# Scatters that no longer wait for each other, and one gather put behind a branch, in the last pairs of a routed expert kernel

## The chip, the cores and the metric

The kernel runs on one core of a Trainium2 chip. The metric is device time in microseconds; the time before is the median of 6 runs. One more execution was profiled, and every reading of the profile below is from that one. TensorE is called PE, VectorE DVE, ScalarE ACT, GpSimd POOL and SyncE SP. "PEld" is PE's loading of weights, and a "q" behind an engine's name (POOLq) means its instruction queue: branches, waits on semaphores, issues of DMAs.

## The reference

The inputs are `x` (8 batches, 8 heads, 512 tokens, 64 wide), a `state` of 32 rows per head, and the weights of 8 experts. First comes a small attention in both directions, which gives 544 rows of 512 per batch:

```python
xread = softmax(x @ state.T * scale) @ state
sread = softmax(state @ x.T * scale) @ x
x = concat([xread, sread])          # (8, 544, 512) after the heads are joined
```

Then every row passes through one of the experts:

```python
logits = x @ w_gate                                  # (8, 544, 8)
local_gate = sigmoid(x @ w_local)
for s in range(S):
    fresh_e = argmax(logits[b, s])
    e = fresh_e if s == 0 or local_gate[b, s] < 0.5 else prev_e
    prev_e = e
    p = softmax(logits[b, s])
    h = max(x[b, s] @ w1[e], 0)                      # 512 -> 1024
    out[b, s] = p[e] * (h @ w2[e])                   # 1024 -> 512
```

There are 4352 rows in all. The change touches only the second part, where rows are gathered by expert, multiplied with that expert's two matrices, and scattered back to their places in `out`.

## The kernel before

The first part of the kernel (the first 130 us or so) computes the attention and the routing: it writes the rows to a DRAM tensor `rows` and works out, on the chip, which row goes to which slot. Slots are dealt to experts in *pairs* of two blocks of 128 rows. How many pairs there are depends on the data; a number between `NPMIN` = 10 and `NP` = 23 is read into a register, `pairs`. Rows that don't fill a pair are handled by small tiles of 32 rows, one beside each of the first nine pairs.

The pairs 0 to 8 are written out as straight code (the loop that calls `pair(u, True, ...)`). From pair 9 on the function `last` takes over: it calls `pair(u, ..., late=False)`, and the next pair stands inside `tc.If(pairs > u + 1)`, so that it runs only if it exists. These are the conditional pairs of this text. With the inputs at hand the 32 scatters of the profile show 16 pairs, so pairs 9 to 15 run in this form; pair 15 is the last, and behind it each engine takes its branch to the end of the kernel.

A pair does two products by a scheme with seven instead of eight block products (a Strassen scheme). The function `seven` writes their order out by hand: products 1, 5, 6, 2, 3, 7, 4 in the second half of a conditional pair (`apart=True`). The first half (`strassen`) makes the hidden layer from the transposed rows `x_t` and the weights `a`; the second half (`second_half`) makes the output from the hidden layer and the weights `c`. PE runs the block products; ACT and DVE copy the results out of PSUM, scale them by the row's probability, and add them up into two output tiles: `ys[0]` for the pair's first 128 rows, `ys[1]` for its other 128.

- `ys[0]` is complete after product 2 (line 1073), and is scattered there, by `scatter(2 * u, ys[0])` in line 1074.
- `ys[1]` is complete after the last product (line 1080). Its scatter is put in the list `behind` (line 1081) and issued by `pair` at its end (lines 1163 to 1165).

Each scatter is an indirect DMA of GpSimd (line 996): 128 rows of 512 floats go to the rows of `out` that `slots.tok` names. The framework tracks what each instruction reads and writes and puts in semaphore waits on its own. All scatters write the same tensor `out`, at places that it can't know, so it makes each wait until the one before has landed.

Gathers, too, are indirect DMAs of GpSimd (line 821, function `quarter`). While pair u is worked on, the rows of later pairs are fetched in quarters of 32 rows: in the first half of pair u the four quarters of the second block of pair u+1 (`getting(u + 1, 1)`), in the second half the four of the first block of pair u+2 (`getting(u + 2, 0)`). To pace them, `seven` calls `gets(value)` after certain products, with a value that ACT has just written. The generator `gathers` first copies one element of it to `tick` (line 835, on GpSimd), which makes GpSimd wait for ACT, and then issues one gather. In the second half of a conditional pair the four values are r5, r2, `ys[0]` after product 1, and `ys[0]` after product 2. So the fourth gather is issued between the first and the second scatter.

In pair u + 1 DVE transposes the gathered rows into `x_t` (line 849), in `ready(0)`, and `ready(1)` closes the second half: two adds of weight blocks on DVE (`first_sums`, line 930, `a<-a,a`). The next pair begins with four adds of `c<-c,c` (`second_sums`). At the border between first and second half of a conditional pair stands a `drain` of GpSimd's queue (line 1154).

Weights come from DRAM by SP's queue (line 873), a quarter of an expert's matrix at a time into a ring of nine buffers.

All order on an engine is the order in which the Python code issues the instructions; no planner reorders them. So GpSimd's order at the end of a conditional pair is: tick and third gather, first scatter, tick and fourth gather, second scatter, the branch of `tc.If` (line 1193), and then the ticks and gathers of the next pair's first half.

Of the kernel before, what the change touches and what calls it, by code (L numbers as in the profile page):

```python
# [23 lines left out]
NT = B * T  # L24
# [9 lines left out]
Q = P // SQ  # L34
# [4 lines left out]
NP = (NT + (E - 1) * (PAIR - 1)) // PAIR  # L39
# [742 lines left out]
def experts(ctx, late, tc, bank, w1, w2, rows, slots, route, routing, out):  # L782
    nc = tc.nc
# [7 lines left out]
    ys = first  # L791
# [20 lines left out]
    def places(u, i):  # L812


        n = 7 * u if u == 0 or i else 7 * u - 3
        (w11, w12, w21, w22), sums = [[ring[i][(n + j) % RING] for j in js] for js in (range(4), range(4, 7))]
        return ((w11, w12), (w21, w22)) if i == 0 else ((w11, w21), (w12, w22)), sums
# [22 lines left out]
    def begun(generator):  # L840
        next(generator)
        return generator
# [20 lines left out]
    def load(u, i, quarters=slice(4)):  # L863

        e = index(slots.experts[0:1, u - 1:u] if u else slots.again if i else slots.expert)
        q = places(u, i)[0]
        for half, other in [((0, 0), (0, 1), (1, 0), (1, 1)), ((0, 0), (1, 0), (0, 1), (1, 1))][i][quarters]:
            to = q[half][other]
            if i:
                w = w2[bass.ds(e, 1), half, :, other]  # L870
            else:
                w = w1[bass.ds(e, 1), half, :, other * KT * F // 4:(other + 1) * KT * F // 4]
            nc.sync.dma_start(out=to.rearrange("p k f -> p (k f)"), in_=w.rearrange("o p x -> (o p) x"))

    class Tile:
# [48 lines left out]
        def scatter(self, y):  # L924
            at = bass.IndirectOffsetOnAxis(ap=slots.row[:, self.k, self.q:self.q + 1], axis=0)
            nc.gpsimd.indirect_dma_start(out=out.rearrange("n (q x) -> (n q) x", q=Q), out_offset=at, in_=y,
                                         in_offset=None, bounds_check=NT * Q - 1, oob_is_err=False)

    def add(out, a, b, op=Alu.add):
        nc.vector.tensor_tensor(out, a, b, op=op)  # L930
# [12 lines left out]
    def first_sums(u, part):  # L943
        ((a11, a12), (a21, a22)), to = places(u, 0)
        if part == 0:
            add(to[0], a21, a22)
            add(to[1], to[0], a11, Alu.subtract)
        else:
            add(a21, a11, a21, Alu.subtract)
            add(to[2], a12, to[1], Alu.subtract)  # L950

    def column_sums():
        sums_of_rows(xq, (xs[0], xs[1], xs[3]), lambda b22, b12: add(xs[2], b22, b12, Alu.subtract))

    def second_sums(u):
        sums_of_rows(*places(u, 1), lambda b22, b12: add(b12, b12, b22, Alu.subtract))

    def seven(y, n, product, copies, whole, gets, waiting=(), apart=False):


        x, v = bank()[:, :n], bank()[:, :n]
        y = y[:, :n]
        product(x, 1, True)
        nc.scalar.copy(y, x)  # L964
        product(v, 5, True)
        five, two, three = copies
        gets(five(v))
        product(y, 6)
        gets(two(y))
        for results in waiting[:1]:  # L970
            results()
        product(x, 2)
        gets(whole(1, x))
        if apart:
            product(v, 3)
            gets(whole(2, v))
            product(y, 7)
            three(y)
            whole(4, None)
            z = bank()[:, :n]  # L980
            product(z, 4, True)
            gets(whole(3, z))
            return
        product(y, 7)
        gets(three(y))
        for results in waiting[1:]:
            results()
        whole(4, None)
        product(v, 3)
        whole(2, v)  # L990
        product(y, 4)
        whole(3, y)

    def scatter(b, y):
        to = bass.IndirectOffsetOnAxis(ap=slots.tok[:, b:b + 1], axis=0)
        nc.gpsimd.indirect_dma_start(out=out, out_offset=to, in_=y, in_offset=None, bounds_check=NT - 1,  # L996
                                     oob_is_err=False)

    def strassen(u, others, gets, waiting):
        ((a11, a12), (a21, a22)), was = places(u, 0)  # L1000
# [41 lines left out]
    def second_half(u, others, ready, gets, behind, late):  # L1042
        ((d11, d12), (d21, d22)), wcs = places(u, 1)
        seconds = {1: (h11, d11), 2: (h21, d21), 3: (hs[2], d22), 4: (h22, wcs[2]), 5: (hs[0], wcs[0]),
                   6: (hs[1], wcs[1]), 7: (c12, d12)}
        r5, r2, r7 = [h1.tile([P, D // 2], F32, name=f"r{i}") for i in range(3)]
        p0, p1 = [slots.prob[:, 2 * u + b:2 * u + b + 1] for b in range(2)]
        low, high = slice(0, D // 2), slice(D // 2, D)

        def second(to, i, begin=False):  # L1050
            x, w = seconds[i]
            for m in range(FK // 2):
                nc.tensor.matmul(to, lhsT=x[:, m, :], rhs=w[:, m, :], start=begin and m == 0, stop=(m == FK // 2 - 1),  # L1053
                                 skip_group_check=True)

        def scaled(to, p):
            def copy(t):
                nc.scalar.activation(to, t, Act.Copy, scale=p)  # L1058
                return to
            return copy  # L1060

        def second_whole(i, t):
            if i == 1:
                others(1)
                scaled(ys[0][:, low], p0)(t)
                ready(0)
                if late:
                    ready(1)
                return ys[0]
            elif i == 4:  # L1070
                add(ys[1][:, high], r7, r5)
            elif i == 2:
                nc.vector.scalar_tensor_tensor(ys[0][:, high], t, p0, r2, Alu.mult, Alu.add)
                scatter(2 * u, ys[0])
                return ys[0]
            else:
                if late:
                    scaled(ys[1][:, low], p1)(t)
                else:
                    nc.vector.scalar_tensor_tensor(ys[1][:, low], t, p1, r7, Alu.mult, Alu.add)  # L1080
                behind.append(lambda: scatter(2 * u + 1, ys[1]))
                return ys[1]

        seven(sums[1], D // 2, second, [scaled(r5, p1), scaled(r2, p0), scaled(r7, p1)], second_whole,
              gets, apart=not late)
        if not late:
            ready(1)
# [21 lines left out]
    def pair(u, ahead=True, tile=None, after=None, waiting=(), late=True):  # L1109


        behind = []
        if ahead:
            for i in range(2):
                load(u + 1, i, slice(2) if u or i else slice(4))
        second_sums(u)
        if tile:
            tile.turned()

        def between():  # L1120
            if u == 0:
                next(probabilities)
            if tile:
                tile.one()
            if after:
                after.load(0)
                after.gather()

        def others(i):

            if ahead:
                load(u + 1, i, slice(2, 4))

        def ready(i):
            if ahead:
                first_sums(u + 1, i)
                if i == 0:
                    turned(u + 1)
                    column_sums()

        def getting(v, b):
            if not ahead or v >= NP:
                return lambda value: None
            generator = begun(gathers(v, b))
            return lambda value: generator.send(value[0:1, 0:1])


        gets = [getting(u + 1, 1), getting(u + 2, 0)]
        if u:
            strassen(u, others, gets[0], waiting)  # L1150
        else:
            plain(u, [getting(1, 0), gets[0]])
        if not late:
            nc.gpsimd.drain()
        between()
        second_half(u, others, ready, gets[1], behind, late)
        if u == 0:
            next(probabilities)
        if tile:
            behind.append(tile.two())  # L1160
        if after:
            after.load(1)
        if not late:
            for results in behind:
                results()
        return behind

    tiles = [Tile(i) for i in range(NTILE)]
# [16 lines left out]
    waiting = ()  # L1185
    for u in range(NPMIN - 1):
        waiting = pair(u, True, tiles[u], tiles[u + 1] if u + 1 < NTILE else None, waiting)

    def last(u, waiting=()):

        pair(u, u + 1 < NP, waiting=waiting, late=False)
        if u + 1 < NP:
            with tc.If(pairs > u + 1):
                last(u + 1)

    last(NPMIN - 1, waiting)


# [31 lines left out]
```

## Time and profile before

| what | value |
|---|---|
| median of 6 runs | 549.3 us (547.45 to 551.52) |
| profiled execution, its own time | 549.46 us |
| its span, first to last instruction | 547.7 us |
| mean clock granted to PE | 0.987 |
| PE busy | 526.9 us (96%) |
| DVE busy | 382.1 us (70%) |
| ACT busy | 174.1 us (32%) |
| POOL busy | 316.8 us (58%) |
| gathers of line 821 | 132, mean 1185 ns |
| scatters of line 996 | 32, mean 1046 ns, 42.2 us of idle time ahead of them |

The page of the profile gives for each engine its busy time as a share of the span. An engine that is busy 96% bounds most of the span, but not every stretch of it: at the start and at the end others do. The span is 1.8 us shorter than the execution's own time, which also holds what lies before its first instruction and after its last.

In a timeline a line holds the start in us from the span's beginning, how long it lasted, the engine, the line of the program, the operation with its tiles, and in square brackets how long the engine stood idle before it and what released it. For a GpSimd DMA the duration is the time in which GpSimd is occupied with issuing it; the data move afterwards. In the chain of waits, a line `DMA out_dram<-y,tok` is the time from the start of such an issue until its data had landed.

### The profile page before, as it was taken

Reading aid. Unit: us, or ns where it says so; the run is one execution under the profiler, and the core shown is the slowest. Engines: PE = TensorE matmul, PEld = TensorE weight load, DVE = VectorE, ACT = ScalarE, POOL = GpSimd, SP = SyncE. Lnnn points to the kernel's source line nnn. Section 1 sums busy time; section 2 is a strip of 40 time slices with the busy share of each in tenths; the row PEclk is TensorE's granted clock in tenths of the full one; section 3 lists DMA queues with packets and bytes.
Section 4 is the critical chain, followed back from the end, with each engine's and each line's share of the span. In section 5 each row is a group of like instructions: output and inputs, shape, how many; then the busy total and the mean of one; then the engine's idle time right before and its main releaser. Section 6 shows DMA issues by size and latency. Waiting matters only on the chain.

```text
span 547.7 us, 12958 instructions
## 1 busy us (share of the span) xinstructions
PE 526.9 (96%) x4916; PEld 460.6 (84%) x4916; DVE 382.1 (70%) x623; ACT 174.1 (32%) x359; POOL 316.8 (58%) x386
## 2 busy tenths in 40 slices
PE   7799898999999999999999999999999999999993
PEld 2567675988989898989898989889999998999992
DVE  6999976748566757475756658485777677787773
ACT  6698754112213122222222121313222222323230
POOL 6788702555574757565646455456554667655564
PEclk9899998899999999999999999999999999999998
DMA  8999866799989899897979798864648474666743
GB/s 315 387 345 359 293 247 217 268 397 377 377 286 382 307 345 351 297 391 281 384 287 373 293 368 299 318 234 152 233 162 284 144 285 153 246 190 234 254 135 105
DMA packets 49003, 155.48 MB, mean 284 GB/s; under 512 B 6865, under 2 KB 8017, under 8 KB 45602
## 3 DMA queue, kind: packets, MB, share of 16 engines
q1 hardware_dynamic: 41234, 135.78, 67.8%
q0 software_dynamic: 7552, 18.69, 9.6%
q8 instruction: 42, 0.69, 0.5%
q14 instruction: 31, 0.25, 0.2%
q10 hardware_dynamic: 144, 0.07, 0.1%
HBM read 136.68 MB, written 17.89 MB: 282 GB/s over the span
## 4 chain that ended last, share of the span: by engine, by line
PE 82%; DVE 6%; DMA 4%; POOL 4%; issue 3%; POOLq 0%; ACT 0%; DVEq 0%
PE ps L1053 21%; PE ps L1013 19%; PE sum L1013 14%; PE sum L1053 12%; PE ps L916 3%; PE ps L904 3%; PE ps L1097 3%; PE p L432 2%; DMA x_n<-in_xn_dram 2%; PE ps L710 2%; POOL xg L821 1%; DMA x_t<-in_xt_dram 1%; PE p L390 1%; PE s L307 1%; DVE a L371 1%
## 5 line engine op out<-in xcount | busy, mean ns | idle before, releaser
L821 POOL DMA_INDIRECT xg<-rows,row x132 | 156.4, 1185 | 28.5 <-issue 27.1
L930 DVE TENSOR_TENSOR a<-a,a 128x1024 f32<-128x1024 f32 x64 | 76.9, 1222 | 23.9 <-DMA a<-in_w_dram 22.5
L1013 PE MATMUL ps<-xt,a 128*128 128x128 f32 x720 | 89.0, 276 | 0.0
L1013 PE MATMUL sum<-xs,a 128*128 128x128 f32 x720 | 87.8, 275 | 0.0
L1013 PEld LDWEIGHTS ps<-xt,a 128*128 128x128 f32 x720 | 84.5, 192 | 2.2 <-issue 1.8
L1013 PEld LDWEIGHTS sum<-xs,a 128*128 128x128 f32 x720 | 84.0, 192 | 0.0
L930 DVE TENSOR_TENSOR c<-c,c 128x1024 f32<-128x1024 f32 x64 | 75.4, 1220 | 4.2 <-DMA c<-in_w_dram 3.7
L1053 PE MATMUL ps<-c,h 128*128 128x256 f32 x312 | 74.7, 382 | 0.0
L1053 PEld LDWEIGHTS ps<-c,h 128*128 128x128 f32 x312 | 58.0, 190 | 10.9 <-issue 3.7
L1053 PE MATMUL ps<-c,hs 128*128 128x256 f32 x256 | 60.5, 379 | 0.0
L996 POOL DMA_INDIRECT out_dram<-y,tok x32 | 33.5, 1046 | 42.2 <-ACT h L1020 13.6
L1053 PEld LDWEIGHTS ps<-c,hs 128*128 128x128 f32 x256 | 48.6, 190 | 6.6
L1053 PE MATMUL sum<-c,h 128*128 128x256 f32 x200 | 47.2, 379 | 0.0
L930 DVE TENSOR_TENSOR h<-s,s 128x512 f32<-128x512 f32 x15 | 10.4, 695 | 49.9 <-ACT s L1036 41.5
L1053 PEld LDWEIGHTS sum<-c,h 128*128 128x128 f32 x200 | 38.0, 190 | 5.2
L835 POOL COPY tick<-s 1x1 f32<-1x1 f32 x45 | 17.1, 381 | 43.0 <-ACT s L1036 42.7
L849 DVE STREAM_TRANSPOSE xt<-xg 128x512 f32<-128x512 f32 x32 | 34.0, 1087 | 6.6 <-DMA xg<-rows,row 6.6
L835 POOL COPY tick<-r 1x1 f32<-1x1 f32 x41 | 19.5, 476 | 32.7 <-ACT r L1058 24.7
L964 ACT COPY sum<-ps 128x256 f32<-128x256 f32 (+1 forms) x31 | 14.3, 461 | 70.9 <-PE ps L1013 52.8
L432 PE MATMUL p<-sd,a 128*128 128x256 f32 x128 | 32.1, 390 | 0.2 <-ACT xr L438 0.2
L1058 ACT ACTIVATE r<-sum,prob 128x256 f32<-128x256 f32 x32 | 15.2, 474 | 52.0 <-PE sum L1053 26.4
L1053 PE MATMUL sum<-c,hs 128*128 128x256 f32 x128 | 30.2, 379 | 0.0
(230 smaller groups left out, 763.6 us busy)
## 6 DMA issues: line engine op xcount, KB each, us to landing
a<-in_w_dram SPq DMA_DIRECT2D x68, 512.0 KB
c<-in_w_dram SPq DMA_DIRECT2D x68, 512.0 KB
at<-in_w_dram SPq DMA_DIRECT2D x18, 1024.0 KB
ct<-in_w_dram SPq DMA_DIRECT2D x18, 1024.0 KB
x_t<-in_xt_dram SPq DMA_DIRECT2D x16, 512.0 KB
x_n<-in_xn_dram SPq DMA_DIRECT2D x8, 1024.0 KB
rows<-xr SPq DMA_DIRECT2D x32, 256.0 KB
xg<-rows,row POOLq DMA_INDIRECT x132
```

Of the source, the lines that this page charges most:

```text
L432: self.nc.tensor.matmul(v[:, d], lhsT=self.get("a", b, u)[:, c * P:c * P + P], rhs=self.sd[:, b, d], start=True, stop=True)
L821: nc.gpsimd.indirect_dma_start(out=to.rearrange("p x k -> p (x k)"), out_offset=None, in_=rows.rearrange("n q x -> (n q) x"), in_offset=ba ...
L835: nc.gpsimd.tensor_copy(tick, value)
L849: nc.vector.transpose(to.rearrange("p k (i t) -> p k i t", i=Q), xgs_[u % 2][:, b].rearrange("p i x k -> p k i x"))
L904: nc.tensor.matmul(hps[SQ * g:SQ * g + SQ, :], lhsT=self.x_t[:, j, :], rhs=a[:, j, :, g], start=(j == 0), stop=(j == KT - 1))
L916: nc.tensor.matmul(yps[SQ * g:SQ * g + SQ, :], lhsT=self.h[:, m, :], rhs=ct_[:, 2 * m // FK, g // 2, m % (FK // 2), g % 2 * P:g % 2 * P + ...
L930: nc.vector.tensor_tensor(out, a, b, op=op)
L996: nc.gpsimd.indirect_dma_start(out=out, out_offset=to, in_=y, in_offset=None, bounds_check=NT - 1, oob_is_err=False)
L1013: nc.tensor.matmul(to[:, m * P:m * P + P], lhsT=w[:, j, m * P:m * P + P], rhs=x[:, j, :], start=begin and m == 0 and j == 0, stop=(m == FK ...
L1053: nc.tensor.matmul(to, lhsT=x[:, m, :], rhs=w[:, m, :], start=begin and m == 0, stop=(m == FK // 2 - 1), skip_group_check=True)
L1058: nc.scalar.activation(to, t, Act.Copy, scale=p)
L1097: nc.tensor.matmul(hps[:, i * P:i * P + P], lhsT=a[n][j // 2][:, j % 2, i * P:i * P + P], rhs=x_t[:, j, b * P:b * P + P], start=(j == 0), ...
```

## The change

Two things are changed, in the conditional pairs only (`late=False`):

- Their scatters are declared to have no dependency on each other. They still wait for their data, and are still waited for by whoever overwrites `ys[0]` or `ys[1]` and by the kernel's end.
- The fourth gather of the second half (of the first block of pair u+2) is not issued after product 2 any more. `pair` returns it as a function, and `last` calls it inside the `tc.If` of the next pair, as the first thing there. It then ticks on `ys[1]` instead of `ys[0]`.

```diff
-    def scatter(b, y):
+    def scatter(b, y, apart=False):
         to = bass.IndirectOffsetOnAxis(ap=slots.tok[:, b:b + 1], axis=0)
-        nc.gpsimd.indirect_dma_start(out=out, out_offset=to, in_=y, in_offset=None, bounds_check=NT - 1,
-                                     oob_is_err=False)
+        put = nc.gpsimd.indirect_dma_start(out=out, out_offset=to, in_=y, in_offset=None, bounds_check=NT - 1,
+                                           oob_is_err=False)
+        if apart:
+            tc.declare_no_dep(put.ins, group="scatters", reason="a token has one slot, so scatters write other rows")
+            tc.add_to_no_dep_group("scatters", put.ins)
...
-                scatter(2 * u, ys[0])
+                scatter(2 * u, ys[0], not late)
...
-                behind.append(lambda: scatter(2 * u + 1, ys[1]))
+                behind.append(lambda: scatter(2 * u + 1, ys[1], not late))
...
         gets = [getting(u + 1, 1), getting(u + 2, 0)]
+        rest = gets[1]
+        if not late:
+            calls = iter(range(NP))
+            gets[1] = lambda value: rest(value) if next(calls) < Q - 1 else None
...
         if not late:
             for results in behind:
                 results()
+            return lambda: rest(ys[1])
         return behind
...
-        pair(u, u + 1 < NP, waiting=waiting, late=False)
+        rest = pair(u, u + 1 < NP, waiting=waiting, late=False)
         if u + 1 < NP:
             with tc.If(pairs > u + 1):
+                rest()
                 last(u + 1)
```

GpSimd's order at the end of a conditional pair becomes: tick and third gather, first scatter, second scatter, branch; and, only if there is a next pair, tick and fourth gather, and then the next pair's own.

## The prediction

> **What bounds the kernel now.** I read the page first (TensorE's row and its slices), then windows cut to single conditional pairs, then the chain that ended last from 536 us on, then the timelines of GpSimd (POOL) and VectorE (DVE) around that end, and the instructions of the branch line and of the kernel's end.
>
> The page, then busy time of the engines in the last conditional pair that ran (stretch, its length, then PE, PEld, DVE, ACT, POOL, with the number of instructions):
>
> ```profile
> span 547.7 us, 12958 instructions
> PE 526.9 (96%) x4916; PEld 460.6 (84%) x4916; DVE 382.1 (70%) x623; ACT 174.1 (32%) x359; POOL 316.8 (58%) x386
> ...
> 513.60:538.40 24.80, 24.77 (x169) 22.96 (x167) 18.26 (x23) 6.41 (x12) 14.63 (x19) 1.00 0.58 205
> ```
>
> PE is busy 24.77 of 24.80 us there, at clock 1.00, and without a gap in the stretches of the five pairs before. Whatever GpSimd waits for inside a pair is hidden; only what lies behind PE's last matmul (538.4) can be won. The chain there, and the groups of the end:
>
> ```profile
> 537.36 3.76 DMA out_dram<-y,tok
> ...
> 541.95 1.02 POOL out_dram L996
> ...
> L1193 DVEq EVENT_SEMAPHORE  x1: 21/21/21, 542.8 to 542.8; - x1
> L1193 POOLq INC_SWDGE_SEM  x1: 316/316/316, 545.8 to 545.8; - x1
> ...
> L1226 PEldq DRAIN  x2: 8/8/8, 542.6 to 547.2; - x2
> L1226 DVEq DRAIN  x2: 10/14/17, 543.1 to 547.1; - x2
> ```
>
> The last scatter starts at 541.95, because the one before (537.36) has to land first. It lands near 541.95 + 3.76 = 545.71, GpSimd goes on at 545.8, the span ends at 547.7. PE and DVE were through at 542.6 and 543.1: the last scatter alone holds the end. Now the two timelines (start, us, what, idle before):
>
> ```profile
> 514.21 2.35 DVE L930 TENSOR_TENSOR a<-a,a 128x1024 f32<-128x1024 f32 x2
> 516.48 4.75 DVE L930 TENSOR_TENSOR c<-c,c 128x1024 f32<-128x1024 f32 x4
> ...
> 538.40 0.48 DVE L1080 SCALAR_TENSOR_TENSOR y<-ps,prob,r 128x256 f32<-128x256 f32 x1 [0.80 <-PE ps L1053]
> 538.80 2.41 DVE L930 TENSOR_TENSOR a<-a,a 128x1024 f32<-128x1024 f32 x2
> ...
> 514.37 1.93 POOL L821 DMA_INDIRECT xg<-rows,row  x1 [0.16 <-issue]
> 520.73 1.39 POOL L996 DMA_INDIRECT out_dram<-y,tok  x1 [4.44 <-DVE c L930]
> ...
> 538.83 0.99 POOL L821 DMA_INDIRECT xg<-rows,row  x1 [0.16 <-issue]
> 541.95 1.02 POOL L996 DMA_INDIRECT out_dram<-y,tok  x1 [2.13 <-DVE a L930]
> ```
>
> The data of the last scatter were ready at 538.40 + 0.48 = 538.88, some 3.07 us before it started. And a DMA that GpSimd issues while DVE adds lasts longer: the gather of 514.37 ended at 516.30, which is 0.91 after the first of the two adds (514.21 + 2.35/2 = 515.39); the scatter of 520.73 ended at 522.12, 0.89 after the last add (521.23).
>
> **The change, part by part.**
>
> *The wait of the second scatter on the first goes.* The built order of POOL's instructions shows it: of `out<-y1`'s waits DVE's stays, that on the first scatter is gone. In the six conditional pairs with a successor, GpSimd stood 3.8 to 5.6 us there in the timelines (4.44 in the last one), and PE's rows show no idle time: worth 0. What is late next on GpSimd is ScalarE's copy of s5 (ends 518.02 in the last pair), then s2, h11 and s7 (ends 523.38). So the four gathers of the first product end near 525 instead of 528.80, the drain at L1154 lets go earlier, and the 0.78 us that DVE's transposition waited at 532.20 goes. All of that lies beside a busy PE: 0.
>
> *In the last pair* the scatter's start is set by DVE: 538.88, not 541.95. Alone it would take 1.02 and end at 539.91, against 542.97: 3.06 us won. But DVE's add starts at 538.80, just ahead of it. Bounds: if the scatter slips through as the gather of 538.83 did (0.99 beside the same adds, starting 0.02 after DVE), it ends at 539.91. If it is held as the gather of 514.37 was (starting 0.16 after DVE), it ends 0.89 after the first add, 538.80 + 1.21 + 0.89 = 540.90. It starts 0.08 or a little more after the add, so between the rows. The nearest is 508.77, a gather 0.10 behind a small add (508.67, 0.42 us), which took 1.18 instead of 0.97 and ended 0.85 after the add: held. I take 540.90: 542.97 - 540.90 = 2.07 us won, and keep 3.06 as the far end. Being held through both adds (541.21 + 0.89 = 542.10, 0.87 won) is the other end; no row shows that, since the gather of 514.37 got through at the first seam.
>
> Landing: the two scatters of before have 3.76 from start to landing and (545.8 for the step that follows the landing) at most 3.85. So +-0.1.
>
> The Trainium skill, SBUF — State Buffer, section "Who interferes with whom", speaks against a held scatter: it reports a `tensor_tensor` as not stalling a DMA of GpSimd, since it takes only the read half of the shared ports. By that rule the scatter would end at 539.91 and the sum would be 3.06; the 1.93 us of the gather at 514.37, beside just such adds, differ from it, and the measurement decides.
>
> *The fourth gather of the second product behind the next condition.* One tick copy (0.18) and one gather (0.97 to 1.93) per pair come after the second scatter and the branch; in the last pair, where the branch is not entered, both are gone (0.18 + 0.99). They ended at 539.82, ahead of the wait that set the end: 0 by themselves, but left in place they would stand before the scatter. In the other six pairs the gather goes out around 517 to 518 instead of 514.4 and is read by a transposition one pair later (about 530): more than 10 us of cover. If that cover were gone, 0.97 us per pair on DVE's chain. The branch costs POOL's queue 0.04 to 0.06. The tick now reads y1, so DVE's next write of y1 gets a wait on GpSimd; it comes some 20 us after that tick. SP's queue and the other engines keep their order.
>
> *Scatters and gathers go out earlier into the weight loads* (DMA share is about 1.0 from 514 to 520): a scatter of 256 KB at the 420 GB/s seen there is 0.6 us for others in the queues. Behind it DVE has idle time (521.23 to 523.41, 2.18 us) and PE reads the new c sums only from 526.11 on. Cost 0; without that cover 0.6 per pair.
>
> *What is behind the scatter*: GpSimd's bookkeeping for skipped DMAs and the closing barrier, 547.7 - 545.71 = 2.0 us, stay. PE (542.6) and DVE (543.1) must not come later than the new landing, 545.71 - 2.07 = 543.64: 0.5 us of room, and more because the barrier asks for DVE late. Their closing branches are slow things: DVE's ran its step behind it only at 542.8, with its last add done at 541.21, and the answer on the branch line has one of 4484 ns on PE's queue.
>
> **Sum**: -2.07, rounded to -2.1 us. The profiled execution took 549.46 us (span 547.7 and 1.8 around it), which gives 547.4. It stands 0.16 above the median of the runs (549.3), so against that median I say 547.2.
>
> **The rivals.**
>
> 1. *The port is free* (the scatter slips past the add): 3.06 won, 546.2. For it: the gather of 538.83, in the same place beside the same adds. Against: it started 0.06 us earlier relative to the add than the scatter can, and the row at 0.10 was held.
> 2. *The end is not the scatter's any more*: PE's and DVE's branch to the closing code (542.6, 543.1) is pushed back by traffic of the earlier scatter, or the scatter is held through both adds. Then 0 to 0.9 is won, 548.4 to 549.3, say 548.9. For it: both are only half a microsecond below the new landing. Against: DVE was ready at 543.1 with the barrier passing only at 547.
> 3. *Slower: weight loads delayed.* In each of the six pairs with a successor the scatter (0.6 us of DMA time) and the gathers behind it (64 KB each, 0.15, three of them) enter the burst of 514 to 520 instead of following it. If c's last quarter or its sums came later by more than DVE's 2.18 us idle and PE's margin (526.11 - 521.23 = 4.9 us), PE would stop. At up to 1.1 us of shift that point isn't reached; were the margin zero, 6 x 1.1 - 2.1 = +4.5, 553.8.
> 4. *The change doesn't do what it says*: the second scatter still waits. The built order speaks against it; it would be 549.3 and is counted with rival 2.
>
> **How the numbers follow.** My forecast 0.62, rival 1 0.17, rivals 2 and 4 together 0.12, rival 3 0.09. Half a per cent (2.7 us) is about what a measurement of this kernel can tell from no change, with runs of before from 547.45 to 551.52. Faster by more than that: about a quarter of the forecast's chance (2.1 won needs 0.65 of luck), 0.16; most of rival 1, 0.13; rival 2, 0.01: 0.30. Slower: nearly all of rival 3, 0.08, and 0.01 of rival 2. The rest, 0.61, is within. Range: 546.2 (rival 1) less 0.8 for the runs' scatter, to 549.3 (no gain) with 0.1: 545.4 to 549.4; the forecast's own range is 546.2 to 548.3.
>
> **What would show it.** PE busy throughout the conditional pairs as before; the last scatter starting within 0.1 us of L1080's end, lasting about 2.0 (held) or 1.02 (free); no gather between the last two scatters; the step after the landing near 543.7 instead of 545.8; the gathers of first products ending 3 to 4 us earlier. Wrong: idle time on PE in a conditional pair, or a span end that follows DVE's or PE's closing instead of the scatter.

## The result, and the profile after

| | before | changed |
|---|---|---|
| median of the runs | 549.12 us (82 runs) | 546.79 us (40 runs) |
| ratio | | 0.9956, 95% interval 0.9944 to 0.9969 |
| span of the profiled execution | 547.7 us | 545.1 us |

The changed kernel is 0.44% faster (0.31% to 0.56%), some 2.4 us (1.7 to 3.1). That is inside the half per cent that the prediction named as "within", at the edge of it, and 0.4 us from the predicted 547.2. Times here and below are medians of all executions; ratios leave out executions more than 1.5% above the fastest of their kernel (one in experiment 2, one of the kernel before in experiments 9 to 11) and are estimates that differ by up to 0.2% from the quotient of the medians beside them.

The page of the changed kernel, its first rows:

```profile
span 545.1 us, 12961 instructions
...
PE 526.9 (97%) x4916; PEld 460.7 (85%) x4916; DVE 382.1 (70%) x623; ACT 174.2 (32%) x359; POOL 321.1 (59%) x384
```

Its last conditional pair (stretch, length, then busy time of PE, PEld, DVE, ACT, POOL):

```profile
513.80:538.60 24.80, 24.76 (x169) 22.96 (x167) 18.20 (x23) 6.41 (x12) 14.53 (x18) 1.00 0.59 215
```

PE does the same work in the same 526.9 us, and is as busy in a pair as before (24.76 of 24.80). The difference lies behind its last matmul. GpSimd's timeline there, first two lines of the kernel before, then the changed kernel:

```profile
527.55 1.25 POOL L821 DMA_INDIRECT xg<-rows,row  x1 [0.16 <-issue]
...
537.36 1.15 POOL L996 DMA_INDIRECT out_dram<-y,tok  x1 [0.30 <-issue]
```

```profile
524.50 0.97 POOL L821 DMA_INDIRECT xg<-rows,row  x1 [0.16 <-issue]
...
536.01 1.02 POOL L996 DMA_INDIRECT out_dram<-y,tok  x1 [0.30 <-DVE y L1076]
539.44 1.73 POOL L996 DMA_INDIRECT out_dram<-y,tok  x1 [2.41 <-DVE y L1083]
```

and DVE's:

```profile
538.68 0.48 DVE L1083 SCALAR_TENSOR_TENSOR y<-ps,prob,r 128x256 f32<-128x256 f32 x1 [0.88 <-PE ps L1056]
539.08 2.35 DVE L930 TENSOR_TENSOR a<-a,a 128x1024 f32<-128x1024 f32 x2
```

Lines have moved by a few: L1083 is the old L1080, L1076 the old L1073, L1056 the old L1053, L1201 the old L1193. The reader sees three things. The last gather of a first product ends at 525.47 instead of 528.80. The first scatter goes out at 536.01 instead of 537.36, now set by its data (L1076) and no longer by a GpSimd that is behind. And the second scatter waits for DVE, not for the first scatter, and lasts 1.73 us instead of 1.02, beside DVE's adds.

Executions begin their pairs up to some 6 us apart (L1083 of the last pair starts between 534.8 and 540.5 in the profiles but one below), so ends are compared from there: from the start of L1083 (L1080) in the last pair to the end of the span. This *tail* was 547.7 - 538.4 = 9.3 us before and is 545.1 - 538.7 = 6.4 us now.

Last, the instructions of the branch line on GpSimd's queue, first of the whole program, then the branch alone out of the stretch from 538 to 541:

```profile
L1201 POOLq COMPARE_BRANCH  x8: 38/39/58, 391.6 to 543.5; - x8
L1201 POOLq EVENT_SEMAPHORE  x5: 17/43/43, 542.8 to 543.1; - x5
L1201 POOLq INC_SWDGE_SEM  x1: 296/296/296, 543.2 to 543.2; - x1
...
L1201 POOLq COMPARE_BRANCH  x1: 58/58/58, 539.2 to 539.2; - x1
```

GpSimd branches at 539.2 and runs its first instruction behind the branch at 542.8, 3.6 us later. The trace has 16 landing records for this scatter; the last of them, with which its data are complete, is at 542.96 (545.74 before). The closing waits on GpSimd follow each other at 0.09 us from 542.8 on, and the one for this scatter is the last of the five, at 543.1: it found the data already there. Behind it stand GpSimd's bookkeeping for skipped DMAs (`INC_SWDGE_SEM`, 543.2) and a second branch (543.5). So landing and branch finish within 0.2 us of each other, and the question for the experiments was which of them sets the end.

### The profile page after: what moved, and what is told of

Its sections match the earlier page's. It is cut to its first block, busy times and chain, and to the rows that moved or that the text cites. A ratio compares the mean times of both kernels' runs of the same rounds, so it can differ in the third digit from the quotient of the medians.

```text
span 545.1 us, 12961 instructions
## 1 busy us (share of the span) xinstructions
PE 526.9 (97%) x4916; PEld 460.7 (85%) x4916; DVE 382.1 (70%) x623; ACT 174.2 (32%) x359; POOL 321.1 (59%) x384
## 4 chain that ended last, share of the span: by engine, by line
PE 89%; DVE 5%; DMA 3%; POOL 1%; issue 1%; ACT 0%; SPq 0%; DVEq 0%
PE ps L1056 23%; PE ps L1016 20%; PE sum L1016 15%; PE sum L1056 13%; PE ps L916 3%; PE p L432 3%; DMA x_t<-in_xt_dram 3%; PE ps L904 3%; PE ps L1100 3%; PE ps L710 2%; PE p L422 1%; PE p L377 1%; PE p L390 1%; PE s L307 1%; DVE a L371 1%
## 5 line engine op out<-in xcount | busy, mean ns | idle before, releaser
L821 POOL DMA_INDIRECT xg<-rows,row x131 | 161.1, 1229 | 30.5 <-issue 29.2
L1056 PE MATMUL ps<-c,h 128*128 128x256 f32 x312 | 74.7, 382 | 0.0
L1056 PEld LDWEIGHTS ps<-c,h 128*128 128x128 f32 x312 | 58.0, 190 | 10.9 <-issue 3.7
L1056 PE MATMUL ps<-c,hs 128*128 128x256 f32 x256 | 60.5, 379 | 0.0
L1056 PEld LDWEIGHTS ps<-c,hs 128*128 128x128 f32 x256 | 48.6, 190 | 6.6
L996 POOL DMA_INDIRECT out_dram<-y,tok x32 | 37.5, 1172 | 27.1 <-DVE y L1083 14.5
L1056 PE MATMUL sum<-c,h 128*128 128x256 f32 x200 | 47.2, 379 | 0.0
L1056 PEld LDWEIGHTS sum<-c,h 128*128 128x128 f32 x200 | 38.0, 190 | 5.2
L835 POOL COPY tick<-s 1x1 f32<-1x1 f32 x45 | 16.0, 356 | 37.2 <-ACT s L1039 37.1
L1056 PE MATMUL sum<-c,hs 128*128 128x256 f32 x128 | 30.2, 379 | 0.0
```

What stands on the lines that cost most here:

```text
L821: nc.gpsimd.indirect_dma_start(out=to.rearrange("p x k -> p (x k)"), out_offset=None, in_=rows.rearrange("n q x -> (n q) x"), in_offset=ba ...
L835: nc.gpsimd.tensor_copy(tick, value)
L996: put = nc.gpsimd.indirect_dma_start(out=out, out_offset=to, in_=y, in_offset=None, bounds_check=NT - 1, oob_is_err=False)
```

## The experiments

Three theories on where the gain is made: A, the prediction's, it is all made by the last pair's second scatter, and the other pairs hide what changes in them; against it, B, each of the seven pairs gives a share, and C, a good part comes from the gather that is gone from the end. Then, on what limits the new end: L, the landing of the last scatter, which the add of DVE would delay by holding its issue; K, GpSimd's branch to the closing code. M, brought up by experiment 2, is that gathers come late. Ratios are against the kernel before on the same chip.

**1. Only the independent scatters.** The gather stays between them.

```diff
-        rest = gets[1]
-        if not late:
-            calls = iter(range(NP))
-            gets[1] = lambda value: rest(value) if next(calls) < Q - 1 else None
...
-            return lambda: rest(ys[1])
...
-                rest()
```

> Only the first part of the change: the scatters of the conditional pairs are independent, the fourth gather stays between them. Theory A (the gain comes from the last pair's second scatter alone, which starts at 539.44 instead of 541.95, and the moved gather gives nothing): in the changed kernel the first scatter of the last pair went out at 536.01, so tick and gather are over by about 538.5, before the second scatter's data are ready at 539.16. 2.3 to 2.7 us below the kernel before. DVE also loses the separate wait ahead of L1083 (0.08 us). Theory C (the gather, left in place, holds the second scatter): 1.0 to 1.7 us below.

Measured: 544.96 against 547.92 us, ratio 0.9941 (0.9919 to 0.9963); tail 543.43 - 536.97 = 6.5 us, the changed kernel's within 0.1. GpSimd's timeline:

```profile
534.38 1.02 POOL L996 DMA_INDIRECT out_dram<-y,tok  x1 [0.30 <-DVE y L1076]
535.38 0.18 POOL L835 COPY tick<-y 1x1 f32<-1x1 f32 x1
535.72 0.99 POOL L821 DMA_INDIRECT xg<-rows,row  x1 [0.16 <-issue]
537.73 1.75 POOL L996 DMA_INDIRECT out_dram<-y,tok  x1 [1.02 <-DVE y L1083]
```

The gather in the middle is over at 536.71, and GpSimd then stands idle for 1.02 us until DVE is ready. C falls: beside independent scatters the moved gather is worth nothing at the end.

**2. Only the moved gather.** The scatters keep their wait.

```diff
-                scatter(2 * u, ys[0], not late)
+                scatter(2 * u, ys[0])
...
-                behind.append(lambda: scatter(2 * u + 1, ys[1], not late))
+                behind.append(lambda: scatter(2 * u + 1, ys[1]))
```

> Only the second part: the fourth gather stands behind the next condition, the scatters still wait for each other. Theory A: the second scatter of the last pair still starts at about 541.9, when the first has landed: within 0.4 us of the kernel before. Theory C (one gather less at the end gives part of the gain): 1 us or more below.

Measured: 552.57 against 547.92 us, ratio 1.0065 (1.0020 to 1.0109). Neither theory had a loss. The profiled execution (546.86 us) was one of the fastest, and shows where it is tight. GpSimd's timeline at the end, and the longest row of DVE's waits from 380 us on:

```profile
536.19 1.12 POOL L996 DMA_INDIRECT out_dram<-y,tok  x1 [0.30 <-issue]
540.33 1.00 POOL L996 DMA_INDIRECT out_dram<-y,tok  x1 [3.02 <-issue]
```

```profile
DVE xt L849 <- DMA xg<-rows,row: 18.9, 7, 3.5
```

and the same row before, then with the whole change:

```profile
DVE xt L849 <- DMA xg<-rows,row: 6.6, 5, 3.1
```

```profile
DVE xt L849 <- DMA xg<-rows,row: 0.7, 1, 0.7
```

Against 6.6 us in 5 waits before and 0.7 us in one wait with the whole change, DVE's transpositions wait 18.9 us for gathers here, up to 3.5 us. The tail is 545.1 - 534.8 = 10.3 us, a full 1.0 longer than before: even the first scatter goes out late, 1.4 us after L1083 has started. But PE has no idle time in this execution's conditional pairs either, so it doesn't show what the slower ones lost.

**3. Both parts, in pair 15 alone** (the last one that runs).

```diff
-                scatter(2 * u, ys[0], not late)
+                scatter(2 * u, ys[0], not late and u == 15)
...
-        if not late:
+        if not late and u == 15:
             calls = iter(range(NP))
```

and so with the second scatter and with the function returned.

> Both parts of the change, but in pair 15 alone, the last one that runs with these inputs. Theory A: the second scatter of the last pair doesn't wait and starts about 0.3 us after L1083's end, near 539.2 to 539.4, is held by the add to about 541: 2.2 to 2.6 us below the kernel before, as with the whole change. Theory B (each of the seven pairs gives its share): about 0.35 us below.

Measured: 544.88 against 547.92 us, ratio 0.9954 (0.9929 to 0.9979), about 2.5 us; tail 543.1 - 536.4 = 6.7 us. One pair gives the whole gain. B falls.

**4. Both parts, in pairs 9 to 14** (`u != 15` in the same places).

> Both parts of the change in pairs 9 to 14 and not in pair 15. The last pair's second scatter waits again for the first. Theory A in its simplest form (only the last pair's own wait counts): the time of the kernel before, within 0.4 us. Theory A with the first scatter's start in it: with pair 14 free of its wait, the drain of pair 15 ends earlier and the first scatter goes out at 536.0 and not 537.4, lands near 539.3, and the second starts at about 540.1, is held by the add to 541.2, with the closing branch about 0.7 us later than in the changed kernel: 1.5 to 2.2 us below. Theory B: 2.0 us below, with the second scatter as late as before.

Measured: 546.73 against 547.92 us, ratio 0.9979 (0.9961 to 0.9996), about 1.15 us (0.2 to 2.1); tail 545.1 - 536.0 = 9.1 us. GpSimd's timeline:

```profile
533.31 1.01 POOL L996 DMA_INDIRECT out_dram<-y,tok  x1 [0.30 <-DVE y L1076]
...
537.66 1.97 POOL L996 DMA_INDIRECT out_dram<-y,tok  x1 [2.02 <-DVE a L930]
```

As expected the first scatter left early (2.7 us before L1083 started, in the kernel before 1.0), landed early, and the second started 1.7 us after L1083 instead of 3.5. But it started 0.1 us into the second add and was held through that one (1.97 us), and by the landing records its data were complete only 5.5 us after its start (12 of the 16 records came within 3.7 us, the last two at 4.6 and 5.5). So the gain is between the two expectations, and the profiled tail shows less of it than the runs; how much the early first scatter is worth by itself stays loose.

**5. The add out of the way.** On the changed kernel, the two adds of `ready(1)` go behind the next condition too, so that none runs beside the last scatter.

```diff
-        if not late:
-            ready(1)
...
-            return lambda: rest(ys[1])
+            return lambda: (ready(1), rest(ys[1]))
```

> The changed kernel with the two adds of first_sums(u + 1, 1) put behind the next condition as well, so that in the last pair no add of DVE runs beside the second scatter. The hold should go in any case: the scatter lasts 1.02 us and not 1.73, its data land 0.7 us earlier. From the start of L1083 to the span's end the changed kernel took 6.4 us (545.1 - 538.68). Theory L (the landing of the last scatter sets the end): 5.7 us. Theory K (GpSimd's branch to the closing code sets it, whose first wait ran only at 542.8, 3.6 us after the branch, with the data in at 543.0): 6.2 to 6.4 us, nothing won.

Measured: 546.88 against 549.72 us, ratio 0.9951 (0.9928 to 0.9975). The scatter in GpSimd's timeline, and the queue's instructions:

```profile
541.30 1.00 POOL L996 DMA_INDIRECT out_dram<-y,tok  x1 [2.41 <-DVE y L1083]
```

```profile
L1199 POOLq EVENT_SEMAPHORE  x5: 17/43/43, 544.7 to 545.0; - x5
L1199 POOLq COMPARE_BRANCH  x2: 38/48/58, 541.1 to 545.4; - x2
```

The hold is gone, 1.00 us instead of 1.73, and nothing is won: tail 546.97 - 540.54 = 6.4 us. The branch at 541.1 has its next instruction at 544.7, again 3.6 us on. And the data were not complete earlier: at 544.84, 3.54 us after the issue began, against 542.96 - 539.44 = 3.52 us in the changed kernel with the hold. So this profile can't tell K from L: the landing (544.84) and GpSimd's wait for it (545.0) come together again.

The 16 landing records say why. Twelve of them came within 2.75 us of the start here, and within 3.42 us in the changed kernel: the hold's 0.7 us later. Counted from the end of the issue the twelfth comes after 1.67 to 1.75 us in all 13 profiles for the last scatter, held or not. It is the last records that stray: the sixteenth comes 0.78 us after the twelfth here, 0.10 in the changed kernel, 1.09 in the kernel before. So the hold does delay most of the data by what it lasts; that nothing was won here came of the last records, and nothing that was tried shows what delays them.

**6. The branch earlier.** The second scatter moves into both arms of the condition, so that GpSimd branches right behind the first scatter.

```diff
-            for results in behind:
-                results()
-            return lambda: rest(ys[1])
+            return behind[0], lambda: rest(ys[1])
...
-        rest = pair(u, u + 1 < NP, waiting=waiting, late=False)
+        put, rest = pair(u, u + 1 < NP, waiting=waiting, late=False)
...
-            with tc.If(pairs > u + 1):
+            with tc.If(pairs > u + 1) as cond:
+                put()
                 rest()
                 last(u + 1)
+            with cond.Else():
+                put()
+        else:
+            put()
```

> The changed kernel with the second scatter in both arms of the condition instead of ahead of it, so that GpSimd branches about 3 us earlier, right behind the first scatter; the adds stay, and hold the scatter. Theory K: the closing code is there when the data land, 6.2 us or less from L1083's start to the end. Theory L: 6.4, as in the changed kernel. A loss is possible if the scatter's own code comes late behind the branch: then the scatter starts later than 0.28 us after L1083's end.

Measured: 544.03 against 549.72 us, ratio 0.9908 (0.9877 to 0.9940). The timeline, and the branches and the bookkeeping on GpSimd's queue between 530 and 543:

```profile
537.87 1.28 POOL L996 DMA_INDIRECT out_dram<-y,tok  x1 [2.86 <-POOLq L1199]
```

```profile
L1199 POOLq COMPARE_BRANCH  x2: 37/48/58, 533.7 to 538.3; - x2
...
L1199 POOLq INC_SWDGE_SEM  x1: 265/265/265, 538.0 to 538.0; - x1
```

The branch is at 533.7, three microseconds ahead of L1083 (536.66). The scatter now waits for GpSimd's queue behind the branch instead of its data: it starts 1.21 us after L1083's start, not 0.76. Even so the tail is 542.4 - 536.7 = 5.7 us, 0.7 less. The landing is no part of that: the last record comes 4.28 us after L1083's start in both kernels. What is shorter is the stretch from the landing to the end, 1.47 us instead of 2.13.

Only some 0.2 of these 0.7 us can be K as it was worded. In the kernel before, GpSimd already stood in the closing code and waited for the landing, and from there to the end took 1.93 us. The other 0.5 us fit what the early branch takes along: `INC_SWDGE_SEM` and the second branch run here at 538.0 and 538.3, ahead of the landing at 540.94, and in the changed kernel behind it. That is read from the order in the traces; it was not tried by itself.

**7. Both edits of 5 and 6.**

> Both of these edits: no hold, and the branch early. If K and L each bind in turn, only this one wins: about 5.5 to 5.7 us from L1083's start to the span's end, 3.2 us below the kernel before instead of 2.4.

Measured: 545.31 against 549.72 us, ratio 0.9922 (0.9894 to 0.9949); tail 544.44 - 538.65 = 5.8 us, as without the adds moved. Nothing shows that the two bind in turn. But little could have shown it: with the scatter starting later in experiment 6, only 0.28 us of the hold was left there, and the last landing record, at 4.28 us after L1083's start there and 4.32 here, hides that much.

**8. The moved gather again**, one more execution of the kernel of experiment 2.

> The kernel of the second experiment (the fourth gather moved, the scatters still waiting) looked at once more. Its executions lay between 546.7 and 555.0 us, and the one that was profiled was among the fastest, with PE busy in all of its pairs and DVE waiting up to 3.5 us for gathers. If the slow ones come from gathers that are late (theory M), an execution above 550 us shows PE idle in some of the conditional pairs, behind a transposition that waited for a gather longer than 3.5 us. If they come from the end of the kernel, PE is busy there as before and the time from L1083 to the end is longer than 10.3 us.

Measured: one execution of 568.79 us (clock 0.97), which is slower than all those of experiment 2. PE's timeline, and the transposition in DVE's ahead of it:

```profile
519.83 1.95 PE L1016 MATMUL ps<-xt,a 128*128 128x128 f32 x16
525.53 3.38 PE L1016 MATMUL ps<-xs,a 128*128 128x128 f32 x16 [3.75 <-DVE xs L930]
```

```profile
523.85 1.08 DVE L849 STREAM_TRANSPOSE xt<-xg 128x512 f32<-128x512 f32 x1 [8.79 <-DMA xg<-rows,row]
```

DVE waited 8.79 us for a gather, its sums `xs` came late, and PE stood idle for 3.75 us in a place where it is never idle in the other profiles (twice, 8.5 us in all). The granted clock, 1.00 in the other stretches of 10 us of these pairs up to 545, was 0.66 and 0.83 in the two where PE resumed after these gaps. So late gathers did stop PE in this execution, as theory M has it. It is one execution, 14 us above the slowest of experiment 2; that late gathers made the 3.6 us of that experiment is likely and not shown, since none of its slower executions was profiled.

**9 to 11. On one chip: the changed kernel, experiment 6 again, and experiment 6 with the gather not moved.** The edit of the last is that of experiment 1 and that of experiment 6 together.

> The changed kernel unaltered, on the same chip as the next two, to compare with them directly: 2.4 us below the kernel before, 6.4 us from L1083's start to the span's end.

> The kernel with the second scatter in both arms of the condition, beside the changed kernel on one chip. Theory K (the early branch saves the time of waiting for the closing code): 0.7 us less from L1083's start to the end, so 3.0 to 3.3 us below the kernel before, about 0.1% below the changed kernel: less than the runs can tell. If the 5 us below the kernel before that it measured were its own, it stays 2 us or more below the changed kernel here.

> Independent scatters, the second in both arms, and the fourth gather where it was, between the scatters (it isn't moved). Theory A and K together: the gather is over before the second scatter's data are ready, so the move is worth nothing: 5.7 us from L1083's start to the end, and the time of the kernel with the move within the runs' uncertainty. Rival (the move helps, by clearing the last pair's end): slower than that one by 0.5 us or more in the time from L1083 to the end.

| kernel | median | ratio to before (548.81) | tail |
|---|---|---|---|
| changed | 546.64 us | 0.9944 (0.9911 to 0.9976) | 6.6 us |
| second scatter in both arms | 545.67 us | 0.9929 (0.9898 to 0.9959) | 5.7 us |
| the same, gather not moved | 545.47 us | 0.9921 (0.9891 to 0.9950) | 5.9 us |

The order is the one that an early branch gives, and the tails are those seen before. The intervals overlap: by time alone the second and third can't be told from the changed kernel, only from the kernel before. The 5 us of experiment 6 did not come again (by the ratio 3.9 of them did, with an interval from 2.2 to 5.6; by the medians 3.1). The move of the gather is again worth nothing that the runs can show; the 0.2 us that its tail is longer without the move rests on one profile each.

**Where the tails differ.** The landing records split each tail in two, at the last scatter's landing (us):

| kernel | L1083's start to the landing | the landing to the end |
|---|---|---|
| before | 7.34 | 1.93 |
| changed; again (9) | 4.28; 4.42 | 2.13; 2.17 |
| independent scatters only (1) | 4.53 | 1.93 |
| last pair only (3) | 4.70 | 1.99 |
| adds behind (5) | 4.30 | 2.13 |
| second scatter in both arms (6; 10) | 4.28; 4.24 | 1.47; 1.47 |
| both arms, adds behind (7) | 4.32 | 1.47 |
| both arms, gather not moved (11) | 4.48 | 1.44 |

The change wins its time in the first column, 2.6 to 3.1 us, and gives back 0.2 in the second: there the closing code comes just after the data, where in experiments 1 and 3 the data come last, as before. The branch in both arms wins 0.7 us in the second column alone, in all four profiles. So L, the landing, sets nearly all of the changed kernel's end, and K, in its narrow sense, the last 0.2 us.

## Why the prediction was right, and where its steps were not

**What bounds the kernel**: right. PE covers the pairs, and the end behind its last matmul is what the change moves; experiment 3 shows it with a single pair.

**The wait goes, 0 in the six other pairs**: right for the change as a whole (experiments 3 and 1 are no slower or faster than it beyond their intervals, and in experiment 3 DVE still waits 6.0 us for gathers). The first products' gathers end 3.3 us earlier, as forecast, and DVE's wait for them falls from 6.6 to 0.7 us. But the cover was called safe with less reason than it looked: experiment 8 shows that late gathers can stop PE, and the wait rows of before (up to 3.1 us, hidden) were the sign. One of the six waits on a first scatter was also longer than the 3.8 to 5.6 us that the prediction read: GpSimd stood idle for 7.1 us ahead of the scatter at 423.94.

**The last scatter, 2.07 us**: right at the end of the issue, by two errors that cancel. From the start of L1083 to the end of the scatter's issue it was 542.97 - 538.40 = 4.57 us before and is 541.17 - 538.68 = 2.49 us now, 2.08 less.

- The start: forecast within 0.1 us of DVE's end. It is 0.28 us behind it (539.16 to 539.44), as it is for every scatter of the changed kernel that waits for DVE (0.30 behind L1076). The rows of before didn't tell this apart from GpSimd's own 0.30 us between a gather and a scatter.
- The hold: forecast, and there, though shorter, 0.71 us instead of 1.0, since the scatter starts 0.36 us into the add and not 0.08. What the Trainium skill (SBUF — State Buffer, "Who interferes with whom") reports from a probe, that a `tensor_tensor` didn't stall a DMA of GpSimd, doesn't hold for these indirect DMAs: against it stand the 1.73 us here and the 1.00 us of the same scatter once the add is gone (experiment 5).
- L1083 itself starts 0.08 us later behind PE (0.88 instead of 0.80). The wait on GpSimd that the tick on `ys[1]` adds is now an instruction of its own on DVE's queue. The prediction saw the wait and gave it no price.

**The landing, 3.76 us after the start, "+-0.1"**: this is the term of the sum that was mis-sized. The prediction read it from two scatters and let the hold add to it what it lasts. For the first twelve of the 16 landing records that is right: they came 1.68 us behind the end of the issue before and 1.69 now. But data are complete with the sixteenth record, and it came 1.09 us after the twelfth before and 0.10 us after it now. So from the issue's end to the landing it was 2.77 us before and is 1.79 now, and the landing came 3.06 us earlier behind L1083 instead of 2.07. Over the kernels with the independent last scatter and its hold (changed, 9, 1, 3) the sixteenth record came 0.10 to 0.48 us after the twelfth, and in experiment 4 it was 1.8 us: no "+-0.1". For the kernel before there is one profile, so how much of its 1.09 us is usual, and what delays the last records, stays open.

**What is behind the landing, "2.0 us, stay"**: nearly right, 1.93 us before and 2.13 now. The 0.2 us are GpSimd's branch, 3.6 us from 539.2 to 542.8, which before lay hidden ahead of the landing (541.7 to 544.4, landing 545.7). The prediction had named slow closing branches, but of PE and DVE (rival 2); those two were through at 541.9 and 542.5:

```profile
L1235 PEldq DRAIN  x2: 8/40/73, 541.9 to 544.6; - x2
L1235 DVEq DRAIN  x2: 10/14/17, 542.5 to 544.5; - x2
```

So the profiled tail is 9.3 - 6.4 = 2.9 us shorter: 2.08 at the end of the issue as forecast, 0.98 more by the last landing records, 0.2 less behind the landing. The runs have 2.4 us, with an interval from 1.7 to 3.1 that holds the forecast 2.1 as well as the 2.9: that the number came out is in part luck, since the terms that were off by 0.2 to 1 us went both ways.

**The fourth gather, 0**: right with the scatters independent (experiments 1 and 11). "Left in place it would stand before the scatter" was wrong: with the first scatter out at 534.4 the gather was over 0.7 us before the data were ready. It alone, with the wait kept, is no zero but a loss of 3.6 us (1.1 to 6.0). That it then stands behind the wait, with everything that follows, fits DVE's 18.9 us of waits, but is argued and not shown as the cause.

**The rivals.** 1, the port is free: the scatter was held. 3, weight loads delayed: no sign of it, PE is not idle in any conditional pair of the changed kernel. 2 looked for a late branch on the wrong engines; GpSimd's was the late one, by 0.2 us. 4: the wait did go.

## What to carry to other kernels

Where one engine covers a stage without a gap, look for what a change is worth behind its last instruction, and write that end down as a race: the landing of the last DMA, the branch to the closing code of each engine, and what an engine still has to run behind the landing. Here it paid to branch early, with the last DMA in both arms: 0.7 us of the tail, too little for the runs to tell. A landing read from one or two profiles isn't sharp: the last of its records moved by up to a microsecond from one profile to the next. A wait on GpSimd's queue that is hidden today still sets when everything queued behind it goes out, so be wary of pushing more work behind it: the moved gather alone cost 3.6 us.

## What was not expected

- A taken branch on GpSimd's queue took 2.64 us to its next instruction before, 3.6 us in the changed kernel and in experiment 5. Moving the branch 3 us ahead of the data, and with it the bookkeeping behind it, took 0.7 us off the tail.
- Of the last scatter's 16 landing records the twelfth comes 1.67 to 1.75 us after the end of the issue in all 13 profiles, whether an add held the issue or not. The sixteenth strays: it came 2.7 to 3.9 us after the issue's start, and 5.5 in experiment 4. What delays it was not tried.
- A scatter starts 0.28 to 0.31 us after the DVE instruction that it waits for.
